# ScalarE's sums for the fourth chunk of x, moved behind the casts of the third chunk's transposition

## The chip, the cores and the metric

The kernel runs on one core of a Trainium2 chip. The metric is the device time of one execution in microseconds (us), the median of several runs. The engines of the core work in parallel, each through its own queue in order: TensorE (PE, with its weight loads shown as PEld), VectorE (DVE), ScalarE (ACT), GpSimd (POOL) and SyncE (SP), which here issues the DMAs.

## The reference

`x` is 2048 tokens of 512 features. What is computed (cut to what matters here):

```python
xn = _layernorm(x, axis=-1)                 # mean and variance over the 512 features of a token
s = _A_ref(xn, A_wqkv, A_wo)                # 32 heads of 16, causal attention in a window of 256 tokens
g = _silu(_B_ref(xn, B_w1, B_b1, B_w2, B_b2))   # layernorm again, 512 -> 1792, GELU, 1792 -> 512
return x + s * g
```

## The kernel before

**Tiling.** The tokens are worked in four chunks of 512 (numbered 0 to 3), each of four tiles of 128 tokens by 512 features. The projections need x normalized and transposed, features on the partitions. Matmuls in full precision are built from a high half (a cast to fp32r) and a low half (the difference), so each transposed bank is emptied in two steps: ACT casts it to the high half, and DVE subtracts that from the bank to give the low half. The result is the tile `xnT` (in the code `big`).

**Slots.** The attention part is one loop over slots `t` from -16 to 64 (lines 775 to 805). Each slot has two halves, in which queued pieces of work ("fills") are issued; between them come steps planned for the slot, and at its end the layernorm steps of `lns`. Every engine takes its instructions in the order in which the program issues them, so where a step stands in this loop is where it stands in its engine's queue. Slots -16 to -1 are the start of the kernel: for chunk `c`, four slots beginning at `4c - 16` hold the q/k projection of the first four heads, a V projection (`pv`), the transposition of chunk `c + 1` and a second V projection (lines 683 to 690). So the third chunk (c = 2) is transposed in slot -10, and the fourth (c = 3) in slot -6. In the same slots the row maxima of scores are taken (`max_block`): PE writes scores to `xy` and `zo`, DVE runs a predicated copy on them and a reduce (`mt`), and PE may write the next scores only when that reduce is done.

**The transposition** of a chunk, lines 237 to 245. A V projection uses the same pair of PSUM banks (`ps_st`) as the first two of the four transposed banks, so it waits until such a bank has been emptied:

```python
239            if i == 0:
240                box.append([fb[0], fb[1], zo[:, 0], None][kt] if c == 1 and kt < 3 else fill_bank() if c > 1 and kt > 1 else
241                           ps_st.tile([P, 512], F32, tag="b", name=f"tr_{c}_{kt}"))
242            nc.tensor.transpose(box[kt][:, P * i: P * (i + 1)], xs[c][i][:, P * kt: P * (kt + 1)], ident)
243            if i == 3:
245                split(big[:, 0, kt, sl], big[:, 1, kt, sl], box[kt])
```

**The layernorm of the fourth chunk** (`ln3`, line 666) is done by sums, three steps for each of the four tiles: `ln3[i][0]` is `total`, `ln3[i][1]` is `squares`, `ln3[i][2]` is `end_sums`. The first two are a pass of ACT over the tile with an accumulated sum, each followed by small steps on POOL; the third is a pass of POOL over the tile:

```python
 92            nc.scalar.activation(x23[:, 8], ts[i], AF.Identity, accum_out=sums[:, i, 0:1])
 93            nc.gpsimd.tensor_scalar(nm[:, i: i + 1], sums[:, i, 0:1], -1.0 / D, None, op0=ALU.mult)
 97            nc.scalar.activation(x23[:, 8], ts[i], AF.Square, bias=nm[:, i: i + 1], accum_out=sums[:, i, 1:2])
 99            nc.gpsimd.tensor_scalar(ve, sums[:, i, 1:2], 1.0 / D, EPS, op0=ALU.mult, op1=ALU.add)
100            nc.gpsimd.tensor_tensor(rs[:, i: i + 1], ve, mhalf[:, :1], op=ALU.pow)
107            nc.gpsimd.tensor_scalar(ts[i], ts[i], nm[:, i: i + 1], rs[:, i: i + 1], op0=ALU.add, op1=ALU.mult)
```

In the profile `nm` is the negated mean, `ve` the variance, `rs` the reciprocal root, and `x<-x` on POOL the scaling of a tile. A wrapper at line 42 issues every operation, so all rows show L42; they are told apart by tile and operation. Other names in the rows: `wqb` are the high and low halves of the next q/k weights (planned for slot -9), `vt` is V as ACT copies it out of `pv`, `sh` the high half of a q/k projection before it is sent to its rows (`qk`) by DMA, `fb` the two banks for q/k projections, and `pt` and `stb` the later softmax's tiles and scores.

The table `lns` (lines 763 to 766) says at the end of which slot each layernorm step of the chunks is issued. Before the change, the fourth chunk's steps stand at slots -11 and -10. The third chunk's transposition lies in slot -10, so the steps of slot -11 stand ahead of its casts on ACT, and those of slot -10 behind them.

Of the kernel before, what the change touches and what calls it, by code (L numbers as in the profile page):

```python
# [49 lines left out]
def mixer_kernel(ctx, tc, x, wqk, wv, wo, w1, b1, w2, b2, out):  # L50
# [615 lines left out]
    ln3 = layernorm(xs[3], "A3", True, True, by_sums=range(4))  # L666
# [93 lines left out]
    def ones():  # L760
# [1 line left out]

    lns = {-16: [ln1[1][1], ln1[0][2], ln1[2][1], ln1[1][2], ln1[3][1], ln2[0][0], ln2[1][0]],
           -15: [ln2[0][1], ln2[2][0], ln2[3][0], ones], -13: [ln2[i][-1] for i in range(4)],
           -11: [ln3[0][0], ln3[1][0], ln3[0][1], ln3[1][1], ln3[2][0], ln3[3][0], ln3[0][2], ln3[1][2]],
           -10: [ln3[2][1], ln3[3][1], ln3[2][2], ln3[3][2]]}

    def fill_in(t, half):
        now[:] = t, half
# [479 lines left out]
```

## Time and profile before

| | us |
|---|---|
| median of 3 runs | 770.04 (769.73 to 770.12) |
| the profiled execution | 769.88 |
| its span, first to last instruction | 768.1 |
| PE busy | 746.0 (97%) |
| DVE busy | 527.0 (69%) |
| ACT busy | 440.1 (57%) |
| POOL busy | 287.0 (37%) |

The mean granted clock of TensorE in the profiled execution is 0.997 of full speed. Times in the views are counted from the start of the span. A row of a timeline has start, duration, engine, operation, output and input tiles with shapes, the number of instructions merged in the row (x24), and in brackets the idle time of the engine ahead of it with what ended it. A row of the waits has who waited for whom, the total, the number of times, and the longest. A row of the windows has the stretch, its length, busy time of PE, PEld, DVE, ACT and POOL with instruction counts, the granted clock, the DMA engines' busy share and GB/s.

### The profile page before, as it was taken

Reading aid. Unit: us, or ns where it says so; the run is one execution under the profiler, and the core shown is the slowest. Engines: PE = TensorE matmul, PEld = TensorE weight load, DVE = VectorE, ACT = ScalarE, POOL = GpSimd, SP = SyncE. Lnnn points to the kernel's source line nnn. Section 1 sums busy time; section 2 is a strip of 40 time slices with the busy share of each in tenths; the row PEclk is TensorE's granted clock in tenths of the full one; section 3 lists DMA queues with packets and bytes.
Section 4 is the critical chain, followed back from the end, with each engine's and each line's share of the span. In section 5 each row is a group of like instructions: output and inputs, shape, how many; then the busy total and the mean of one; then the engine's idle time right before and its main releaser. Section 6 shows DMA issues by size and latency. Waiting matters only on the chain.

```text
span 768.1 us, 18803 instructions
## 1 busy us (share of the span) xinstructions
PE 746.0 (97%) x7428; PEld 583.2 (76%) x7428; DVE 527.0 (69%) x839; ACT 440.1 (57%) x746; POOL 287.0 (37%) x586
## 2 busy tenths in 40 slices
PE   9799999999999999999999999999999999999997
PEld 8787666676768887676676688888878888888886
DVE  7686777777777678887874447863657675676473
ACT  7736766767676676777877755444645553442001
POOL 6411666756565554766776800030101100001102
PEclk9999999999999999999999999999999999999999
DMA  8513355645547863455744283541202322253531
GB/s 284 182 44 70 90 120 136 163 106 137 113 92 208 257 208 100 106 152 135 191 130 148 65 285 123 181 151 51 74 28 89 103 86 85 78 163 121 169 96 55
DMA packets 56951, 99.40 MB, mean 129 GB/s; under 512 B 11104, under 2 KB 11360, under 8 KB 56864
## 3 DMA queue, kind: packets, MB, share of 16 engines
q1 hardware_dynamic: 56864, 98.21, 44.5%
q8 instruction: 58, 0.95, 0.5%
q14 instruction: 29, 0.24, 0.1%
HBM read 51.39 MB, written 29.62 MB: 105 GB/s over the span
## 4 chain that ended last, share of the span: by engine, by line
PE 87%; ACT 5%; DVE 4%; issue 2%; POOL 2%; DMA 1%; SPq 0%; DVEq 0%; ACTq 0%; POOLq 0%
PE acc L42 19%; PE fb L42 18%; PE zo L42 13%; PE p L42 9%; PE stb L42 8%; PE h L42 6%; PE s L42 6%; PE xy L42 5%; ACT pt L42 3%; PE pv L42 2%; POOL pt L42 1%; DVE xy L42 1%; ACT x L42 1%; DVE mt L42 1%; PE yt L42 1%
## 5 line engine op out<-in xcount | busy, mean ns | idle before, releaser
L42 POOL TENSOR_SCALAR_AFFINE_SELECT pt<-pt 128x256 f32<-128x256 f32 x480 | 192.8, 426 | 164.2 <-ACT pt L42 161.7
L42 ACT ACTIVATE pt<-stb 128x768 f32<-128x768 f32 (+1 forms) x244 | 188.6, 773 | 55.7 <-PE stb L42 46.0
L42 DVE TENSOR_REDUCE mt<-xy 128x4 f32<-128x1024 f32 (+1 forms) x128 | 152.6, 1193 | 4.4
L42 PE MATMUL acc<-w,gh 128*128 128x512 f32 x432 | 134.7, 393 | 0.0
L42 DVE COPY_PREDICATED xy<-upper,zo 128x512 f32<-128x512 int32 x112 | 77.6, 693 | 69.1 <-PE zo L42 68.4
L42 PE MATMUL fb<-xnT,wqb 64*128 64x512 f32 (+1 forms) x684 | 115.2, 404 | 0.9 <-DVE xnT L42 0.9
L42 PE MATMUL zo<-pt,vt 128*17 128x128 f32 x2880 | 103.7, 275 | 1.8 <-DVE xy L42 1.2
L42 PE MATMUL stb<-qk 64*128 64x384 f32 (+1 forms) x488 | 96.9, 393 | 7.3 <-ACT pt L42 5.3
L42 POOL TENSOR_TENSOR xo<-xo,gated 128x512 f32<-128x512 f32 x15 | 20.1, 1346 | 219.0 <-DVE gated L42 195.3
L42 PEld LDWEIGHTS zo<-pt,vt 128*17 128x17 f32 x2880 | 67.5, 97 | 38.7 <-issue 18.0
L42 PEld LDWEIGHTS acc<-w,gh 128*128 128x128 f32 x432 | 80.9, 188 | 17.2
L42 PEld LDWEIGHTS stb<-qk 64*128 64x128 f32 x488 | 45.5, 183 | 53.1 <-ACT pt L42 42.2
L42 PE MATMUL acc<-w,gl 128*128 128x512 f32 x216 | 84.3, 390 | 0.0
L42 PEld LDWEIGHTS fb<-xnT,wqb 64*128 64x128 f32 (+1 forms) x684 | 63.4, 186 | 7.9 <-DVE xnT L42 1.3
L42 PE MATMUL xy<-qk 64*128 64x256 f32 (+2 forms) x536 | 61.6, 304 | 1.7 <-DVE mt L42 1.5
L42 ACT COPY oraw<-zo 128x128 f32<-128x128 f32 x128 | 34.1, 266 | 40.2 <-PE zo L42 36.3
L42 PEld LDWEIGHTS xy<-qk 64*128 64x128 f32 x536 | 43.9, 185 | 12.8 <-DVE mt L42 6.3
L42 PEld LDWEIGHTS acc<-w,gl 128*128 128x128 f32 x216 | 40.5, 188 | 9.3 <-DVE gl L42 0.2
L42 ACT ACTIVATE gated<-acc 128x512 f32<-128x512 f32 x16 | 8.7, 596 | 65.0 <-DVE acc L42 65.0
L42 PE MATMUL s<-wos,ohl 128*128 128x512 f32 (+1 forms) x204 | 44.8, 378 | 0.0
L42 PEld LDWEIGHTS s<-wos,ohl 128*128 128x128 f32 x204 | 36.7, 188 | 7.1
L42 ACT COPY p<-p 128x512 f32<-128x512 f32 x21 | 12.3, 584 | 50.1 <-PE p L42 42.6
(190 smaller groups left out, 1191.8 us busy)
## 6 DMA issues: line engine op xcount, KB each, us to landing
qk<-sh SPq DMA_DIRECT2D x128, 128.0 KB
qk<-pjr SPq DMA_DIRECT2D x64, 128.0 KB
oT_d<-oraw SPq DMA_DIRECT2D x32, 256.0 KB
w_d<-in_w_dram SPq DMA_DIRECT2D x14, 512.0 KB
x<-in_x_dram SPq DMA_DIRECT2D x16, 256.0 KB
or<-oT_d SPq DMA_DIRECT2D x16, 256.0 KB
w<-rden_d SPq DMA_DIRECT2D x16, 256.0 KB
xo<-in_x_dram SPq DMA_DIRECT2D x16, 256.0 KB
```

Of the source, the lines that this page charges most:

```text
L42: r = issue(*args, **kwargs)
```

## The change

The steps of the fourth chunk leave slot -11. The totals, squares and scalings of tiles 0 and 1 are issued at the end of slot -10, those of tiles 2 and 3 at the end of slot -9. Nothing else is changed; the number of instructions of each engine stays the same.

```diff
     lns = {-16: [ln1[1][1], ln1[0][2], ln1[2][1], ln1[1][2], ln1[3][1], ln2[0][0], ln2[1][0]],
            -15: [ln2[0][1], ln2[2][0], ln2[3][0], ones], -13: [ln2[i][-1] for i in range(4)],
-           -11: [ln3[0][0], ln3[1][0], ln3[0][1], ln3[1][1], ln3[2][0], ln3[3][0], ln3[0][2], ln3[1][2]],
-           -10: [ln3[2][1], ln3[3][1], ln3[2][2], ln3[3][2]]}
+           -10: [ln3[0][0], ln3[1][0], ln3[0][1], ln3[1][1], ln3[0][2], ln3[1][2]],
+           -9: [ln3[2][0], ln3[3][0], ln3[2][1], ln3[3][1], ln3[2][2], ln3[3][2]]}
```

## The prediction

> **What bounds the kernel now.** I began with the page, to see which engine sets the span and which engine the chain that ended last runs through.
>
> ```profile
> span 768.1 us, 18803 instructions
> ...
> PE 746.0 (97%) x7428; PEld 583.2 (76%) x7428; DVE 527.0 (69%) x839; ACT 440.1 (57%) x746; POOL 287.0 (37%) x586
> ...
> PE 87%; ACT 5%; DVE 4%; issue 2%; POOL 2%; DMA 1%; SPq 0%; DVEq 0%; ACTq 0%; POOLq 0%
> ```
>
> PE (TensorE) is busy in 746.0 of 768.1 us, and 87% of the chain is its work. All that can be won without removing matmuls is the 22 us in which it stands idle. So the next view is what PE waited for, over the whole run, and beside it what DVE (VectorE) waited for between 28 and 40 us.
>
> ```profile
> PE stb L42 <- ACT pt L42: 5.3, 14, 1.0
> PE pv L42 <- DVE xnT L42: 3.3, 1, 3.3
> ...
> DVE xnT L42 <- ACT xnT L42: 3.3, 1, 3.3
> ```
>
> The longest single wait of PE in the kernel is 3.3 us: a V projection (pv) waits for DVE's low half of the transposed x (xnT), and DVE in turn waits for ACT's (ScalarE's) cast to the high half. The chain that ended last runs through this very place:
>
> ```profile
> 34.02 0.48 ACT xnT L42
> 34.52 0.70 DVE xnT L42
> 35.27 4.63 PE pv L42 x24
> ```
>
> The busy time by windows shows what the stall does to PE, the clock included:
>
> ```profile
> 32.00:35.30 3.30, 0.03 (x1) 0.03 (x1) 0.78 (x2) 3.24 (x9) 2.67 (x7) 1.00 0.01 3
> 36.00:40.00 4.00, 4.00 (x23) 3.86 (x23) 3.77 (x5) 2.05 (x6) 2.99 (x6) 0.57 0.02 4
> ```
>
> In the first stretch PE is busy 0.03 us of 3.30 while ACT is busy 3.24. In the second PE is always busy, but at a granted clock of 0.57. The share of the DMA engines in both is 0.01 and 0.02: nothing that was sent or fetched before is still on the way here.
>
> **What ACT does in the stall.** PE and ACT in order of time (start, duration, what; xnT casts are the ones that PE's chain needs):
>
> ```profile
> 25.57 3.13 PE L42 MATMUL pv<-wva,xnT 128*128 128x256 f32 x24
> 28.64 0.50 PE L42 MATMUL xy<-qk 64*128 64x256 f32 x4
> 29.07 1.09 PE L42 MATMUL tr<-ident,x 128*128 128x128 f32 x8
> 30.00 1.04 PE L42 MATMUL fb<-ident,x 128*128 128x128 f32 x8
> ...
> 31.59 0.33 PE L42 MATMUL zo<-qk 64*128 64x128 f32 x4
> 35.27 4.63 PE L42 MATMUL pv<-wva,xnT 128*128 128x256 f32 x24 [3.34 <-DVE xnT L42]
> 39.83 0.50 PE L42 MATMUL xy<-qk 64*128 64x256 f32 x4
> ...
> 40.44 1.66 PE L42 MATMUL fb<-xnT,wqb 128*128 128x512 f32 x6
> 42.56 0.50 PE L42 MATMUL xy<-qk 64*128 64x256 f32 x4 [0.47 <-DVE mt L42]
> ...
> 48.33 0.60 PE L42 MATMUL tr<-ident,x 128*128 128x128 f32 x4
> ```
>
> ```profile
> 28.74 0.59 ACT L42 COPY vt<-pv 128x512 f32<-128x512 f32 x1 [1.90 <-PE pv L42]
> 29.22 0.63 ACT L42 ACTIVATE x<-x 128x512 f32<-128x512 f32 x1
> ...
> 30.79 0.72 ACT L42 ACTIVATE x<-x,nmA 128x512 f32<-128x512 f32 x1
> ...
> 32.55 0.63 ACT L42 ACTIVATE x<-x 128x512 f32<-128x512 f32 x1
> ...
> 33.93 1.05 ACT L42 CAST xnT<-tr 128x512 fp32r<-128x512 f32 x2
> ...
> 35.82 0.75 ACT L42 ACTIVATE x<-x,nmA 128x512 f32<-128x512 f32 x1
> ...
> 37.48 0.60 ACT L42 CAST wqb<-wqkr 128x512 fp32r<-128x512 f32 x1
> ...
> 44.86 0.59 ACT L42 CAST sh<-fb 128x512 fp32r<-128x512 f32 x1 [4.33 <-PE fb L42]
> ```
>
> PE has finished the third chunk's transposition at 31.04 (30.00 + 1.04). The casts that empty its banks start only at 33.93, because ACT takes its instructions in order and six sums of the fourth chunk stand ahead of them (29.22 to 33.93). The V projection needs the first of those banks and so cannot begin.
>
> **The change, part by part.** It adds and removes no instruction. The instruction order of the changed kernel shows, on ACT behind the third V copy: four xnT casts, two totals and two squares of the fourth chunk, the cast of the next q/k weights (wqb), the fourth V copy, then the other two totals and squares. On PE, DVE and SP the order stays. On POOL the scaling of the fourth chunk's first two tiles moves ahead of the last two negated means.
>
> *The four casts.* They now start as the banks are transposed: the first at 30.16 at the latest (29.07 + 1.09), the last just behind 31.04. Four take 1.89 us when they queue (33.93 to 35.82), so ACT is free of them at about 31.6 (the last starts near 31.1 and holds ACT a quarter of 1.89). DVE now decides when the subtractions begin:
>
> ```profile
> 29.97 1.23 DVE L42 TENSOR_REDUCE mt<-xy 128x4 f32<-128x1024 f32 x1
> 34.52 1.29 DVE L42 TENSOR_TENSOR xnT<-tr,xnT 128x512 fp32r<-128x512 f32 x2 [3.33 <-ACT xnT L42]
> ...
> 36.92 0.69 DVE L42 COPY_PREDICATED xy<-upper,zo 128x512 f32<-128x512 int32 x1
> 37.65 1.23 DVE L42 TENSOR_REDUCE mt<-xy 128x4 f32<-128x1024 f32 x1
> 38.79 1.02 DVE L42 TENSOR_TENSOR wqb<-wqkr,wqb 128x512 fp32r<-128x512 f32 x1
> 40.55 0.70 DVE L42 COPY_PREDICATED xy<-upper,zo 128x512 f32<-128x512 int32 x1 [0.74 <-PE zo L42]
> 41.28 1.23 DVE L42 TENSOR_REDUCE mt<-xy 128x4 f32<-128x1024 f32 x1
> ```
>
> Behind a reduce the next operation follows 1.14 after its start (37.65 to 38.79), so the first subtraction starts at 31.1 instead of 34.52. Before, PE followed 0.75 behind that start (34.52 to 35.27); that gives 31.85, and PE itself is free at 31.92 (31.59 + 0.33). The V projection starts at 31.92 instead of 35.27: 3.35 us earlier, the stall gone whole.
>
> *The V projection itself.* Its 24 matmuls took 4.56 us here (35.27 to 39.83), and 3.07 (25.57 to 28.64) for the same work a stage before. The difference of 1.49 lies in the stretch with the clock at 0.57. Without the idle stretch I expect 3.07: PE is done at 34.99, 4.84 us earlier than 39.83.
>
> [...]
>
> *What is late next: DVE.* Its four subtractions take 2.40 (34.52 to 36.92), so from 31.1 the predicated copy starts at 33.5, the reduce 0.73 later at 34.23, and ends at 35.46. PE's next scores (the ones at 39.83) wait for that reduce and start 0.05 behind its end (41.28 + 1.23 = 42.51, scores at 42.56): 35.51. So PE waits 0.5 us for DVE, and the gain here is 39.83 - 35.51 = 4.3.
>
> *The weights' cast, in its new place.* Two totals and two squares took 3.33 us (29.22 to 32.55). From 31.6 that ends at 34.93; the wqb cast takes 0.60, to 35.53. DVE's subtraction of wqb stands behind the reduce and ahead of the next predicated copy, for which PE then waits. It could start at 35.37 (34.23 + 1.14) and starts at 35.55; it takes between 0.65 (a half of the pair of 1.29) and 1.02 (its own row), so it ends between 36.2 and 36.57. The predicated copy is possible 0.72 behind PE's scores (39.83 to 40.55), at 36.23. I take 36.45, nearer to its own row: 40.55 - 36.45 = 4.1. From there copy, reduce and scores follow as before: the scores at 42.56 come at about 38.5. The six q/k matmuls between (1.66 in 40.44) end by 37.8 and hide under it.
>
> Those scores read the q and k rows of the second chunk, which come by DMA and do not move. The DMA share of 0.01 from 32.00 to 35.30 says that they have landed by then, so they set nothing at 38.5.
>
> *The other two sums.* They move behind the fourth V copy, which now ends near 35.95: PE done at 35.05 (31.92 + 3.13), the copy queued behind the wqb cast's end, 0.59. Two totals take 1.57 (29.22 to 30.79). Their squares need negated means from POOL, which now stand behind the scaling of the first two tiles:
>
> ```profile
> 34.10 0.21 POOL L42 TENSOR_SCALAR nmA<-sumsA 128x1 f32<-128x1 f32 x1 [0.46 <-ACT x L42]
> ...
> 38.51 1.95 POOL L42 TENSOR_SCALAR x<-x,nmA,rsA 128x512 f32<-128x512 f32 x2
> ```
>
> Scaling followed 2.69 behind the start of its squares (35.82 to 38.51). The first squares start at 33.2 (31.6 + 1.57), their scaling at 35.9 and ends by 37.8 (1.95). A first negated mean of 0.21 lets the squares start at 38.05; ACT is free 1.66 later (35.82 to 37.48) at 39.7, and the last scaling runs from 40.75 to 42.7. Two things wait for these: the cast at 44.86, now due at 40.75, and the fourth chunk's transposition at 48.33, due at 44.2. Covers of 1.0 and 1.5 us; beyond them each us late costs one.
>
> *Sum.* 4.1 us earlier from 38.5 on. What follows runs through the same orders and is set by PE and DVE. The profiled execution took 769.88 us (span 768.1 and 1.78 around it), 0.16 under the median of 770.04. 769.88 - 4.1 + 0.16 = **765.9 us**.
>
> **Rivals.** *The clock falls anyway.* Suppose the half clock does not hang on the gap. Then the V projection takes 4.56 from 31.92, to 36.48, later than DVE's 35.51; the gain is 3.35 and the time 766.7. [...] Against it: the stretch that follows the one long gap is the one with 0.57. 7%.
>
> *ACT is the next stall.* DVE's wqb subtraction waits for a cast behind four sums, and PE waits behind that. Each us by which the sums take longer than 3.33, or the casts end later than 31.6, is lost. With 1 to 2 us lost the time is 766.9 to 767.9. For it: the cast is already the later of the two by 0.16. Against it: 3.33 contains the same round through POOL. 8%.
>
> *The gain is used up later.* Something with a fixed time takes the shift back: 770.0. The one candidate is a transfer, and DMA's share of 0.01 in the stall speaks against it. 4%.
>
> *Slower: the fourth chunk comes late.* Its transposition waits for the last scaling on POOL. From 35.95 to 42.7 that batch takes 6.75 us; it decides from 44.2 on, and makes the kernel slower than before from 48.33 on. If POOL and ACT kept each other waiting so that it took 2.2 times that, 14.85, it would end at 50.8, and the transposition would run 2.5 us later than before: 772.5. For it: totals, negated means, squares and scaling go to and fro between two queues, and the means now stand behind 1.95 us of scaling. Against it: that wait is in the 6.75 already. 4%.
>
> That the change does not do what it says I rule out: the instruction order shows the casts directly behind the V copy.
>
> **How the numbers follow.** The forecast has 77% and gives 765.4 to 766.4: DVE's wqb subtraction between its two ends moves it by 0.35, the times of the casts by a few tenths more. 0.2%, about what a measurement of this kernel can tell from no change, is 1.5 us: faster means below 768.5. Faster: forecast, clock and ACT cases, 77 + 7 + 8 = 92%. Same: 4%, slower: 4%. The range goes down to 764.9: PE's own 4.84, if DVE set nothing, gives 765.2, and the runs shown lie up to 0.3 under their median (769.73 to 770.12, median 770.04). It goes up to 767.3, which holds the clock case and about half of the ACT case.
>
> **What would show it.** Right: PE's wait of 3.3 for xnT is gone, the V projection starts near 31.9 and takes 3.1, the clock holds 1.00 from 32 to 40; PE has two waits of 0.5 to 0.8 for DVE before 39; the fourth chunk's transposition lies near 44.2. Wrong: a half clock near 36 (second case), a gap on DVE before the wqb subtraction (third), transposes waiting for POOL (slower case), or a shift of 4 at 60 us that is smaller at the end (fourth).

## The result and the profile after

The changed kernel takes 766.0 us (median of 6 runs, 765.62 to 766.73), the kernel before 770.08 (median of 6 runs, 769.65 to 771.3): a ratio of 0.9947 to the kernel before, 95% interval 0.9934 to 0.9959, or 4.1 us less. The forecast was 765.9.

The page of the profiled execution (765.62 us), and of PE's waits over the whole run the two with the largest totals:

```profile
span 763.9 us, 18803 instructions
...
PE 744.6 (97%) x7428; PEld 581.6 (76%) x7428; DVE 526.7 (69%) x839; ACT 440.2 (58%) x746; POOL 287.1 (38%) x586
...
PE 88%; DVE 5%; ACT 4%; issue 2%; POOL 1%; DVEq 0%; ACTq 0%
```

```profile
PE stb L42 <- ACT pt L42: 5.7, 15, 1.0
PE xy L42 <- DVE mt L42: 2.0, 6, 0.5
```

PE's wait of 3.3 us for the low half of xnT is off the list. In its place the waits for DVE's reduce (mt) have grown from 1.5 us in 5 waits to 2.0 in 6. PE's busy time fell by 1.4 us with the same 7428 matmuls, about the 1.5 us by which the V projection got shorter (4.63 to 3.13). The windows show both:

```profile
32.00:36.00 4.00, 3.48 (x34) 3.21 (x32) 3.88 (x6) 3.79 (x11) 1.54 (x6) 1.00 0.11 26
36.00:40.00 4.00, 3.54 (x25) 2.70 (x26) 3.75 (x7) 3.38 (x9) 3.16 (x7) 1.00 0.00 0
```

PE is busy 3.48 and 3.54 us of 4, and the granted clock is 1.00 in both. From here on times are better compared as distances. The scores ahead of the third chunk's transposition start at 29.10 here and at 28.64 before, and at 28.3 to 29.8 in the runs below; the start of the kernel varies by that much between executions.

The stage itself, by PE, ACT, DVE and POOL in order of time:

```profile
29.10 0.50 PE L42 MATMUL xy<-qk 64*128 64x256 f32 x4
...
32.06 0.34 PE L42 MATMUL zo<-qk 64*128 64x128 f32 x4
32.32 3.13 PE L42 MATMUL pv<-wva,xnT 128*128 128x256 f32 x24
35.97 0.51 PE L42 MATMUL xy<-qk 64*128 64x256 f32 x4 [0.52 <-DVE mt L42]
...
38.70 0.50 PE L42 MATMUL xy<-qk 64*128 64x256 f32 x4 [0.46 <-DVE mt L42]
...
44.47 0.60 PE L42 MATMUL tr<-ident,x 128*128 128x128 f32 x4
```

```profile
30.23 1.07 ACT L42 CAST xnT<-tr 128x512 fp32r<-128x512 f32 x2 [0.43 <-PE tr L42]
...
32.14 0.67 ACT L42 ACTIVATE x<-x 128x512 f32<-128x512 f32 x1
...
35.38 0.60 ACT L42 CAST wqb<-wqkr 128x512 fp32r<-128x512 f32 x1
...
38.33 0.72 ACT L42 ACTIVATE x<-x,nmA 128x512 f32<-128x512 f32 x1 [0.50 <-POOL nmA L42]
...
40.99 0.59 ACT L42 CAST sh<-fb 128x512 fp32r<-128x512 f32 x1 [0.94 <-PE fb L42]
```

```profile
30.44 1.23 DVE L42 TENSOR_REDUCE mt<-xy 128x4 f32<-128x1024 f32 x1
31.58 1.28 DVE L42 TENSOR_TENSOR xnT<-tr,xnT 128x512 fp32r<-128x512 f32 x2
...
36.01 0.69 DVE L42 TENSOR_TENSOR wqb<-wqkr,wqb 128x512 fp32r<-128x512 f32 x1
36.69 0.70 DVE L42 COPY_PREDICATED xy<-upper,zo 128x512 f32<-128x512 int32 x1
```

```profile
36.39 1.70 POOL L42 TENSOR_SCALAR x<-x,nmA,rsA 128x512 f32<-128x512 f32 x2
38.07 0.41 POOL L42 TENSOR_SCALAR nmA<-sumsA 128x1 f32<-128x1 f32 x2
...
40.97 1.54 POOL L42 TENSOR_SCALAR x<-x,nmA,rsA 128x512 f32<-128x512 f32 x2
```

The casts start when the transposition gives them something (30.23), and ACT is the one that waits, 0.43 us, for PE. DVE goes from its reduce straight to the subtractions (31.58), and the V projection follows the scores without a gap (32.32). From the scores ahead of the transposition to the second scores behind the V projection it took 13.92 us before (28.64 to 42.56), and takes 9.60 now (29.10 to 38.70): 4.32 less. The experiments below give this as the distance between the scores.

### The profile page after: what moved, and what is told of

The parts are those of the page before. It is cut to its first block, busy times and chain, and to the rows that moved or that the text cites. A ratio compares the mean times of both kernels' runs of the same rounds, so it can differ in the third digit from the quotient of the medians.

```text
span 763.9 us, 18803 instructions
## 1 busy us (share of the span) xinstructions
PE 744.6 (97%) x7428; PEld 581.6 (76%) x7428; DVE 526.7 (69%) x839; ACT 440.2 (58%) x746; POOL 287.1 (38%) x586
## 4 chain that ended last, share of the span: by engine, by line
PE 88%; DVE 5%; ACT 4%; issue 2%; POOL 1%; DVEq 0%; ACTq 0%
PE acc L42 19%; PE fb L42 18%; PE zo L42 14%; PE p L42 9%; PE stb L42 8%; PE h L42 6%; PE s L42 6%; PE xy L42 5%; ACT pt L42 3%; PE pv L42 2%; DVE xy L42 1%; POOL pt L42 1%; DVE mt L42 1%; DVE xnT L42 1%; PE yt L42 1%
## 5 line engine op out<-in xcount | busy, mean ns | idle before, releaser
L42 ACT COPY oraw<-zo 128x128 f32<-128x128 f32 x128 | 34.1, 266 | 40.2 <-PE zo L42 36.2
```

The source lines that it names most:

```text
L42: r = issue(*args, **kwargs)
```

## The experiments

**Fill the gap, first try.** The kernel before, with matmuls of its own in PE's idle stretch.

```diff
     def fill_in(t, half):
         now[:] = t, half
+        if (t, half) == (-9, 0):
+            for _ in range(24):
+                nc.tensor.matmul(zo[:, 0, 256:384], ident, ident, start=True, stop=True)
```

> The kernel before, with 24 small matmuls of its own (ident times ident, into a part of the PSUM tile zo that nothing reads) put ahead of the V projection that waits; they fill 2.7 to 2.9 us of PE's 3.34 us of idling and add no work to any other engine. Theory (the half clock belongs to the idle stretch): the clock stays at 1.00 from 36 to 40 us, the V projection takes 3.1 us instead of 4.6, and since DVE's reduce ahead of the next scores ends at 38.88 and its wqb subtraction at 39.81, only 0.8 of the 1.49 us reach the end: 769.2. Rival (the half clock comes at that place whatever PE did before): the V projection takes 4.6 us again, and the time stays at 770.0.

778.99 us, ratio to the kernel before 1.0113 (1.0098 to 1.0128): neither of the two expected times.

```profile
38.83 8.01 PE L42 MATMUL zo<-ident 128*128 128x128 f32 x48 [5.75 <-DVE xy L42]
46.59 3.11 PE L42 MATMUL pv<-wva,xnT 128*128 128x256 f32 x24
```

```profile
40.00:44.00 4.00, 4.00 (x22) 4.00 (x21) 0.98 (x2) 0.00 (x0) 1.62 (x2) 0.52 0.00 0
```

The added matmuls write `zo`, and the predicated copy queued on DVE reads `zo`: they waited for it, so the gap grew to 5.75 us instead of being filled. They also took 8.0 us: each is two instructions (x48), twice what the expectation counted with, and they ran mostly at half clock (0.52). As a test of the clock it fails, but it gives one reading: with a gap of 5.75 us the clock goes to half again.

**Fill the gap, second try.** The same at a place where nothing holds the matmuls up, and half as many:

```diff
         for fn, args in fills.get((t, half), ()):
             fn(*args)
+        if (t, half) == (-10, 1):
+            for _ in range(12):
+                nc.tensor.matmul(zo[:, 1, 384:512], ident, ident, start=True, stop=True)
```

> The kernel before, with 12 matmuls of its own (ident times ident into a part of zo that nothing reads) put ahead of the scores of slot -10, so that they wait for nothing: they run in the idle stretch for about 2.8 us and leave some 0.5 us of it. ACT, DVE and POOL have the same work in the same order. Theory (the half clock belongs to the idle stretch): the clock stays at 1.00 from 36 to 40 us, the V projection takes 3.1 us instead of 4.6; DVE's reduce ahead of the next scores ends at 38.88 and its wqb subtraction at 39.81, so 0.8 of the 1.49 us reach the end: 769.2. Rival (the half clock comes at that place whatever PE did before): 4.6 us again and 770.0.

769.58 us, ratio 0.9991 (0.9982 to 1.0001). Its PE and window rows:

```profile
28.67 0.50 PE L42 MATMUL xy<-qk 64*128 64x256 f32 x4
...
30.91 2.84 PE L42 MATMUL zo<-ident 128*128 128x128 f32 x24
...
35.31 3.14 PE L42 MATMUL pv<-wva,xnT 128*128 128x256 f32 x24 [0.95 <-DVE xnT L42]
38.97 0.50 PE L42 MATMUL xy<-qk 64*128 64x256 f32 x4 [0.52 <-DVE mt L42]
...
41.77 0.51 PE L42 MATMUL xy<-qk 64*128 64x256 f32 x4 [0.54 <-DVE mt L42]
```

```profile
36.00:40.00 4.00, 3.48 (x31) 3.16 (x30) 3.96 (x6) 2.62 (x6) 2.95 (x6) 1.00 0.00 0
```

With 2.84 us of matmuls in the gap, of which 0.95 us is left, the clock stays at 1.00 and the V projection takes 3.14 us, though ACT and DVE are as late as in the kernel before. So the half clock did belong to the idle stretch. This holds beyond the profiled execution: the mean granted clock of all ten executions is 0.999 to 1.000, that of the fifteen of the kernel before beside them 0.995 to 0.997. The distance between the scores is 13.10 us (28.67 to 41.77) against 13.92: 0.82 less, the 0.8 of the expectation. The interval of the time itself just reaches no change. The half clock alone thus cost the kernel before 0.8 us, not 1.49: the rest was hidden behind DVE, which is as late there.

**Half of the change.** Tiles 0 and 1 stay ahead of the casts:

```diff
+           -11: [ln3[0][0], ln3[1][0], ln3[0][1], ln3[1][1], ln3[0][2], ln3[1][2]],
+           -9: [ln3[2][0], ln3[3][0], ln3[2][1], ln3[3][1], ln3[2][2], ln3[3][2]]}
```

> Half of the change: tiles 0 and 1 stay ahead of the third chunk's casts (slot -11), tiles 2 and 3 go to slot -9. On the time scale of the kernel before, the casts start at 32.55 instead of 33.93, the first subtraction at 33.1, the V projection near 33.9: PE is idle for 2.0 us instead of 3.34. Theory with the clock holding: the reduce ends at 37.5, the scores at 39.83 come at 37.55, 767.7 us in all. Theory with the clock falling in a gap of 2 us too: the V projection ends at 38.45, 768.6 us. Rival (the sums ahead of the casts all count, or none): 766.0 or 770.0.

768.12 us, ratio 0.9974 (0.9964 to 0.9984).

```profile
34.12 3.13 PE L42 MATMUL pv<-wva,xnT 128*128 128x256 f32 x24 [1.84 <-DVE xnT L42]
```

In the profiled execution (767.72 us) the gap is 1.84 us and the V projection takes 3.13. Four sums ahead of the casts instead of six leave 1.84 us of the gap; none ahead leave nothing. The time falls between the two kernels, and that of the profiled execution is what was worked out for a clock that holds (767.7). But the nine executions are of two kinds: five with a mean granted clock of 0.998 to 1.000 took 767.72 to 768.12 us, four with 0.996 to 0.997 took 768.56 to 769.32, which is where a fallen clock was expected (768.6) or a little more. No trace shows where those four ran at half clock; the last section comes back to this.

**Five sums ahead.** As above, with `ln3[2][0]` moved into the list of slot -11.

> As with half of the change, but with a third total ahead of the casts too, so that PE's idle stretch is 1.84 + 0.76 = 2.6 us. Where does the clock fall? If it holds at 2.6 us: 768.1 + 0.8 = 768.9. If it falls: the V projection takes 4.6 us and the time is 769.5 to 769.8.

One run, 768.8 us.

```profile
35.20 3.13 PE L42 MATMUL pv<-wva,xnT 128*128 128x256 f32 x24 [2.60 <-DVE xnT L42]
```

```profile
36.00:40.00 4.00, 3.48 (x30) 3.15 (x29) 3.79 (x6) 1.95 (x5) 0.21 (x1) 1.00 0.02 4
```

A gap of 2.60 us, and the clock holds, in the one execution that there is.

**All sums at slot -10.** Behind the third chunk's casts, but all ahead of the weights' cast:

```diff
+           -10: [*[ln3[0][0], ln3[1][0], ln3[0][1], ln3[1][1], ln3[0][2], ln3[1][2]],
+                 *[ln3[2][0], ln3[3][0], ln3[2][1], ln3[3][1], ln3[2][2], ln3[3][2]]]}
```

> All twelve steps of the fourth chunk at the end of slot -10: behind the third chunk's casts as in the changed kernel, but all ahead of the cast of the next q/k weights. Theory (DVE's in-order queue waits for that cast, and PE for DVE): the cast ends near 40.7 instead of 36.0 on the changed kernel's time scale, the predicted copy starts at 41.4 instead of 36.7, and the kernel takes 766.0 + 4.7 = 770.7 us, more if the clock falls in the new gap of PE. Rival (the weights' cast has slack, only the casts of the third chunk count): 766.0.

772.35 us, ratio 1.0026 (1.0015 to 1.0037): slower than before the change.

```profile
40.52 0.69 DVE L42 TENSOR_TENSOR wqb<-wqkr,wqb 128x512 fp32r<-128x512 f32 x1 [4.51 <-ACT wqb L42]
```

```profile
43.13 0.80 PE L42 MATMUL xy<-qk 64*128 64x256 f32 x4 [4.81 <-DVE mt L42]
...
46.90 2.38 PE L42 MATMUL pv<-wva,xnT 128*128 128x256 f32 x12
```

```profile
44.00:48.00 4.00, 4.00 (x16) 3.30 (x15) 2.16 (x3) 0.59 (x1) 0.00 (x0) 0.50 0.03 4
```

The third chunk's casts are as early as in the changed kernel, and still all is lost: DVE stands 4.51 us for the cast of weights that no matmul needs before slot -2 (line 692 plans their first use, `job_qk(1, 0)`, there), because its subtraction is queued ahead of the predicated copy for which PE waits. PE's gap of 4.81 us then brings the half clock (0.50), the part that the 770.7 left open ("more if the clock falls"): the same 12 matmuls take 2.38 us instead of 1.58 in the kernel before and 1.60 in the changed one. So the split of the sums in two slots is as much a part of the gain as their place behind the casts.

**One slot later.** Slots -9 and -8:

```diff
+           -9: [ln3[0][0], ln3[1][0], ln3[0][1], ln3[1][1], ln3[0][2], ln3[1][2]],
+           -8: [ln3[2][0], ln3[3][0], ln3[2][1], ln3[3][1], ln3[2][2], ln3[3][2]]}
```

> Both halves of the change one slot later still (slots -9 and -8). Theory (the fourth chunk's transposition has a cover of 1.5 to 2 us ahead of it, and what exceeds it is lost one to one): the weights' cast comes early and wins nothing; the last scaling on POOL ends near 47.3 instead of 42.5, the transposition due at 44.5 begins its third tile then, and the kernel takes about 766.0 + 2.7 = 768.7 us. Rival (the later, the better, since ACT has idle time after 40 us): 766.0 or less.

768.01 us, ratio 0.9979 (0.9967 to 0.9992): 2.0 more than the changed kernel.

```profile
46.16 0.33 PE L42 MATMUL tr<-ident,x 128*128 128x128 f32 x1 [1.67 <-POOL x L42]
46.91 0.77 PE L42 MATMUL tr<-ident,x 128*128 128x128 f32 x5 [0.42 <-POOL x L42]
```

The fourth chunk's transposition waits 1.67 and 0.42 us for POOL's scaling of the third and fourth tile, 2.09 in all, and the time is 2.0 longer. The price is as expected in kind, and 0.7 lower. The last scaling ended where I had it (46.85, with the stage 0.36 earlier than in the changed kernel: 47.2 on its scale), but I let the third tile's transposes wait for it as well, which need only their own tile. The earlier cast of the weights won nothing: the distance between the scores is 9.60 us here too (28.74 to 38.34).

**DVE reordered.** The changed kernel, with the low halves of banks 2 and 3 behind the predicated copy and reduce, and the subtraction of wqb from slot -9 to -7:

```diff
+                if c == 2 and kt > 1:
+                    nc.scalar.copy(big[:, 0, kt, sl], box[kt])
+                    later(1, lambda: nc.vector.tensor_sub(big[:, 1, kt, sl], box[kt], big[:, 0, kt, sl].bitcast(F32)))
+                    return
                 split(big[:, 0, kt, sl], big[:, 1, kt, sl], box[kt])
...
-        at(t, split_wqk, 1)
+        at(-7 if n == 1 else t, split_wqk, 1)
```

> The changed kernel with two of DVE's steps moved behind what PE waits for: the low halves of the third chunk's banks 2 and 3 go behind the predicated copy and reduce of slot -10, and the subtraction of the next q/k weights goes from slot -9 to slot -7. Theory (after the change DVE sets the scores near 36 us): the scores at 35.97 start right behind the V projection at 35.4, PE's first wait of 0.52 for DVE goes, the second of 0.46 stays since copy and reduce must follow the scores; 0.55 us less than the changed kernel, 765.45. Rival (something else is as late as DVE): 766.0.

> The changed kernel itself, beside the variant with DVE's steps moved, so that the two are compared on the same chip: 766.0 us.

765.35 us, ratio to before 0.9939 (0.9926 to 0.9951); the changed kernel beside it 766.45, 0.9946 (0.9934 to 0.9959).

```profile
28.29 0.50 PE L42 MATMUL xy<-qk 64*128 64x256 f32 x4
...
31.51 3.13 PE L42 MATMUL pv<-wva,xnT 128*128 128x256 f32 x24
34.57 0.50 PE L42 MATMUL xy<-qk 64*128 64x256 f32 x4
...
37.30 0.51 PE L42 MATMUL xy<-qk 64*128 64x256 f32 x4 [0.47 <-DVE mt L42]
```

PE's first wait for DVE is gone and the second stays, as expected. The distance between the scores is 9.01 us (28.29 to 37.30) against 9.60: 0.59 less. So DVE was what set this stage after the change.

The gain of the stage does not reach the end, though. From the scores ahead of the transposition to the end of the span it is 734.9 us in this variant (28.29 to 763.2) and 735.0 in the changed kernel beside it (29.84 to 764.8). At 205.73 us the 0.59 is gone: the same matmuls stand 177.4 us behind those scores here and in the changed kernel (at 207.24 there). In this variant PE's waits for DVE's predicated copy (`xy`) grow from 1.3 us in 4 waits to 1.7 in 5, and a wait for a DMA of q and k rows appears that the changed kernel does not have:

```profile
PE zo L42 <- DVE xy L42: 1.7, 5, 0.6
...
PE stb L42 <- DMA qk<-sh: 0.4, 1, 0.4
```

```profile
205.73 0.85 PE L42 MATMUL zo<-pt,vt 128*17 128x128 f32 x24 [0.41 <-DVE xy L42]
```

The profiled executions, 764.94 and 766.48 us, differ by the 1.55 us between their starts (28.29 and 29.84). So the lower median, whose interval overlaps with the other's, does not show a faster kernel: of the expectation, the theory holds for the stage and the rival (something else is as late) for the whole.

## Why the prediction was right

*The stall goes whole.* Right: the V projection starts 0.26 behind the scores ahead of it (32.06 to 32.32), and 3.22 us behind the start of the scores at 29.10; before it was 6.63 (28.64 to 35.27).

*The clock.* Right: 3.13 us instead of 4.63, at 1.00. The second filler run shows that the gap was the cause of the half clock, and what that was worth by itself: 0.8 us. The case in which the clock falls anyway is refuted.

*DVE is next.* Right: PE waits 0.52 and 0.46 us for DVE's reduce; 0.5 to 0.8 were named, so the second is just under. Moving two of DVE's steps takes the first wait away.

*The weights' cast and subtraction.* The one term that was mis-sized. I let the subtraction end at 36.45, between 36.2 and 36.57 and nearer to its own row of 1.02 us. It took 0.69 and ended at 36.70, which is 36.24 on the scale of the prediction (the scores started 0.46 later here). The row of 1.02 (38.79 to 39.81) was one in which POOL was scaling two tiles at the same time (38.51 to 40.46). So the predicated copy came 0.2 us earlier than I had it, and the stage won 4.32 us rather than 4.1.

*The other two sums.* Right within 0.5: the last scaling ends at 42.51, 1.96 us ahead of the transposition at 44.47 (I had 1.5), and ACT waits 0.94 us for PE ahead of the cast at 40.99 (I had 1.0). The wait of 0.50 for a negated mean queued behind POOL's scaling is there and lies inside this cover. With one slot more the cover is gone, and the excess is lost one to one (2.09 us of waits, 2.0 us of time).

*The shift is kept.* Right: from the scores after the stage to the end of the span it is 725.5 us before (42.56 to 768.1) and 725.2 after (38.70 to 763.9). Nothing took it back. The span is 4.2 shorter, as the stage's 4.32 less the start that was 0.46 later in this execution, and 0.3 that came from elsewhere and that I have not followed. That the forecast of 765.9 meets the median of 766.0 to 0.1 us is therefore luck in part: the stage won 0.2 more than in the sum, 0.3 came on top, and the start of the kernel varies by more than both between executions.

*The rivals that did not come.* ACT as the next stall and the late fourth chunk are both real mechanisms with room between them: the experiments with all sums at slot -10 and with one slot later fell into one and the other, at 772.35 and 768.01 us.

## What to carry to other kernels

Where an engine works in order, look at what stands ahead of the step that the bound engine waits for, and move what has slack behind it; then look at what that work now stands ahead of, for the gain can be lost entirely at a cast that nothing seems to need (all sums at slot -10). The room for such a move has two ends, both readable in the profile of before: the next step on the same engine that another queue waits for, and the due time of the moved work's own reader. A long gap on TensorE is to be looked at together with the matmuls behind it: behind the 3.34 us here the V projection took 4.63 us instead of 3.13. But they count only as far as another engine that is as late does not hide them: 0.8 us here.

## What the runs showed of the hardware

*The clock and the length of a gap.* In the profiled executions the granted clock stayed at 1.00 with gaps of PE of 1.84 and 2.60 us, and went to half with gaps of 3.34, 4.81 and 5.75 us. In the kernel before, the mean of 0.57 from 36.00 to 40.00 makes 3.4 us at half clock, with the rest at 1.00; it was back near 39.7, so it fell near 36.2, some 4.3 us behind the beginning of the gap (31.92), when PE had been busy again for 0.9 us:

```profile
36.50:39.50 3.00, 3.00 (x16) 3.00 (x15) 2.96 (x4) 1.49 (x5) 2.49 (x6) 0.50 0.00 0
39.50:40.00 0.50, 0.50 (x5) 0.36 (x5) 0.31 (x1) 0.06 (x1) 0.50 (x1) 0.82 0.00 0
```

With the gaps of 4.81 us (all sums at slot -10, first row) and 5.75 us (first filler run, second row) the half clock lasted about twice as long (6.7 us in these windows, against 3.4):

```profile
41.90:48.60 6.70, 5.47 (x22) 4.77 (x23) 4.35 (x7) 0.59 (x1) 0.71 (x1) 0.50 0.02 2
```

```profile
37.10:43.80 6.70, 4.97 (x23) 4.98 (x24) 3.84 (x5) 2.05 (x6) 3.45 (x6) 0.50 0.01 2
```

But the length of the gap alone does not sort these executions, and 2.60 us is no safe length. PE also stands idle for the last 4.6 us of the span, in the kernel before (763.55 to 768.1) as in the changed one (759.32 to 763.9) and in half of the change (761.42 to 766.0). There the clock fell 1.9 us behind the end of PE's last matmul in the trace of half of the change (761.42 to 763.3), 4.4 us behind it in the changed kernel (759.32 to 763.7); with five sums ahead the mean clock of the whole execution is 1.0 (0.9995 at the least), so that a fall there lasted 0.8 us at most. The last matmuls and the end of the span in the trace of half of the change:

```profile
760.30 1.12 PE L42 MATMUL s<-wos,ohl 128*128 128x256 f32 x8
```

```profile
763.40:766.00 2.60, 0.00 (x0) 0.00 (x0) 0.00 (x0) 0.00 (x0) 0.00 (x0) 0.50 0.25 88
```

And four of the nine executions of half of the change had a mean clock of 0.996 to 0.997, as low as the 34 executions of the kernel before that ran beside the experiments (0.995 to 0.997). The fall at the end costs the mean 0.002 in the trace in which it came earliest of these (2.7 us at half clock in 766.0), so it does not explain these. That in these four the clock fell with the gap of 1.84 us is likely and not shown.

*VectorE and GpSimd.* In this stage the subtraction of wqb took 1.02 us in the kernel before and 1.03 in the first filler run, where POOL was already scaling a tile (38.79 behind 38.51, 39.95 behind 39.67). It took 0.69 where it came first (36.01 ahead of 36.39 in the changed kernel, 40.52 ahead of 40.90 with all sums at slot -10) and 0.68 with no scaling beside it (half of the change, one slot later). In these rows it took longer where it came second. (In the run with DVE reordered it took 0.69 though the second tile of POOL is recorded 0.06 us ahead of it, at 40.76; that tile then took 1.32 us, against 0.77 for one alone.) In the kernel before, POOL's second tile in that stretch took 1.20 us:

```profile
39.26 1.20 POOL L42 TENSOR_SCALAR x<-x,nmA,rsA 128x512 f32<-128x512 f32 x1
```

DVE's subtraction ended at 39.81 there. In the changed kernel DVE was first (36.01 to 36.70), kept its 0.69, and POOL's pair of tiles took 1.70 instead of 1.54. Why it takes longer there no run shows. But the row of POOL beside the 1.02 us was there to be read in the trace of before, and would have spoken for the lower of the two ends of the prediction, 0.65, which is nearer to the 0.69 measured.
